# A cross network on one core: six full products ahead of a table-driven run of row products, and output stores cut in four and spaced

## The chip, the cores and the metric

The kernel runs on one core of one Trainium2 chip. A time is device microseconds (us) of one execution. The time before is the median of three runs; beside it stands one execution that was taken with the hardware profiler, and all rows below are from that one.

Engines are named as the profile names them. PE is the matrix engine and PEld its weight loads. DVE is the vector engine, ACT the activation engine, POOL the general one. SP issues the DMA transfers and is in order: a transfer that waits for something holds all transfers behind it.

## The reference, cut to what matters

```python
B, F, D, L = 16384, 26, 16, 6
Din = F * D                      # 416
def reference(x0, ws, bs):       # x0 [16384, 416], ws [6, 416, 416], bs [6, 416], bf16
    x = x0
    for l in range(6):
        proj = jnp.einsum('bd,de->be', x, ws[l]) + bs[l]
        x = x0 * proj + x
    return x
```

Each of six layers is a 416 x 416 product over 16384 rows, a bias, a multiplication by the input and an addition.

## The kernel before, in words

**Tiles.** The 16384 rows are eight groups of 2048; a group is four chunks of 512 rows. Activations lie turned: features on the partitions, batch rows along the free side. 416 features are three tiles of 128 and a rest of 32, the tail. One job is a (group, layer) pair; a job has three output tiles of four chunks, and a tail. One output chunk of 128 x 512 in one PSUM bank sums over 416 features: three times 128 and once 32.

**Two ways to multiply.** A full product (`full`, L694) has 128 feature rows, 128 output features and 512 batch columns. A row product (in `stream`, L1153 and, for the last 32 features, L1157) has 32 feature rows in one of four row quarters of the array, at `tile_position=(r*32, 0)`. Four row products, one in each quarter, run side by side and go to four different banks. A chunk needs 13 of them: three in each quarter, and one more in the quarter that holds the chunk's tail.

**The first part.** Up to the tile `s_lo`, which is tile 1 of job (0, 2), tiles are made with full products and a few short ones (`first_job`, `two_tiles`, `full`, `rows32`).

**The run.** From `s_lo` on everything is one searched order, the string `ORDER`. Each letter says which of the chunks in work (its age) gets its turn in which row quarter; that turn is then all the row products of this chunk in this quarter, three or four. `replay` walks the string in ticks, 20 to a row product (`SLOT`), and gives each row product a place in PE's order and each chunk a bank. It holds model costs: how long a bank is read (`READ`, `NEXT`, `BACK`), and when each of the eight banks is free at the start (`banks`). The last four chunks of the run (`keep`) begin the last job's outputs, which are made in natural layout. `|` in the string is a tail block: the tails of three jobs at once (L741 x36 and L729 x12, two jobs in the last one), there are 15 of them.

**Evictions.** When a chunk is complete, ACT moves it from PSUM to a `tw` buffer with the bias (L595); there are four `tw` buffers of four chunks. For each pair of chunks DVE multiplies by x0 (L607) and adds x (L615). Tails go through ACT (L661) or DVE (L657), and then two short DVE operations (L663, L665). L665 of some jobs adds a copy of the old tail that has been moved by some quarters (`prefill`, `rotate`: two DMA transfers, L487 and L488, put on SP's queue when the tail block one layer earlier has been written out).

**Output and input of groups.** When job (g, 5) is done, `output` turns its tiles back by DMA transposes (L945, L952) into one buffer `ost`, POOL spreads the tail (L980), and `store` (L987) sends the whole group, 1664 KB, to memory in one transfer. The transposed tail of a newly loaded group, `Tb`, lies in the same buffer, so its load (L438) waits for the store. `load_group` is called for groups 5, 6 and 7 from the list `later` at the end of the tail block after which the group's buffers come free; for groups 6 and 7 two thirds of the load (L427, eight transposes) are issued with the output already. After `Tb` come four more transposes (L427), four copies out of `Tb` (L462), and a moved copy of the result (L487, L488).

Of the kernel before, what the change touches and what calls it, by code (L numbers as in the profile page):

```python
# [5 lines left out]
T32 = 32  # L6
# [15 lines left out]
class Program:  # L22
# [192 lines left out]
ORDER = (
    "ABCDMBCTZOELBaAjZSIfFiQPVKHYBCcTVIDSJATKBQLWBQXKNALCZQLWBQCbMRLWBITWBQPCZMLWRALSBQLCRIbCRAPeJYWH"
    "N|AWPJQGDQBDWNITCJnQCZTIWBLQWNALWBQXCNIDWZIDWJYTCRbIWBLQBSbINWHAVCTUBOQLBaTARaDQZOLUSBDUORbICJbA"
    "aVTMGBPYBWPIRaHAORDYKBXQKBTIWBDUOZITCZIOTFADeRYPCNIbWQFPK|ABPWAVKPQBCPQVKDAVePQBKfMRaHJAbSIBKTAZ"
    "SLcNHCBQXBSMLBaAOXZQKHMVSDBQOXBMKXAVKDQVKDBMebUJOHAVObIRCLQBSfJ|EODBTAOZACbVcPKFAeXRYGPBYWPRAKPQ"
    "BiLMRGDNACbNAaXNISHBYCTNYCbVISPFAePBUKDVQaDRIOXFAOXBAObVQGLBcCXNAePZIWTFASPBcKPRUGDNAWDNQXCJAbWR"  # L220
    "APSJYDaRUDSJUfOF|ITCRIODJAbSJATJCQDOBPcWJDIeVbQOFXAVODUKBXQKBTIBaLQCZTAOQZLWFPAWNDUCNTUBOTIBaLQN"
    "WALVCQXBOQLBaTINWDIVODUCNXAOJXAWJDUeYBXOIZHSUBTOIBbCMZDWIZTO|EBPWQBOLAVCPQVKfMFSDARWPANXCUNSDIBS"
    "XYBTKAReLMVSbIBKTAhSLYNHCBQXNCMLWBAaPQVKDQBaPBUKjMZSXEBSPAZKPQVHCBQWDMRKXBIWDVAOXJAWfYJTCQZOLEBW"
    "DcRCTMJWbERKP|ABPWQBKPAVCPQVKDANebUBKXQNaHJASXIBKTAhSLYNHCBQXNCMLWBAaXQNKHAZWTMBKDYRKXNAWDNQXBOQ"
    "BObIRWDQBOTICfZAXaRIPFCYPBaUPCMVaLBIWDVQCPRICfJAebJUSPFAaPQVGL|MBDSNAPKBAObRUGLBAeXNYKHVAWTJAKTY"
    "BLCYRWDRIOXBIWPBUOLRAKbBAWPZQCLRYCbNIWTBISPBYKPRAeDQVPKAJXCURCPQJaDIBafQVGPBMaXRIOH|ABTOAZKPQBKD"
    "BUPaAVKbQdCbMRWLEBWTARKPYBWDNQKDZISXBIOTBAOfRYKDZQLWBQKXARKXMBWLBQCPZAWbJQGDQZWPBIWPQBOLAVCPQVKj"
    "MFSDARWPANXCUNSLEBSDYRCTIBafIVOTE|BPWRALOBcDOZQKXBIDVaITCRIbBSYLBSIXNaALVOQDKBQXKBITBaQLVOADOZXA"
    "WJAXSJYDSJYXOFQDZOAXBOQXBOQLBaITVCQDSZMLWBIXSBQLOBIbCZQLCZITWBQLBaITNWALVCUTBSATNaIDJWYTBSPAdOXY"
    "SF|AODVPAKNYXCBQXaJcHORAPaRIHCBUbCRMLWBIWTBQKPVALWRMGDBQCbRMWLBAWbNAKPZUCXQJaPBIWPBcKPVAWLMRCLBQ"  # L230
    "XCRMLWFAWTBQCPZAaPJAWbJMSDZcPCNXYSF|AOTBPAaBYSPJUGDdQODJMbWBIXOdAXKNQHCBQWDMRCbJAaTVIODJAfaUBXSc"
    "NKHAZSXIBLCVYLSNEXCMBWPIBWLAVCXQBOTAdaPUBOLQVaHJAbCMZSLUBSLARKfARWLMBKDYRCPRIbWBQXJOALBaQVCPISXB"
    "ASPYVKHMBCbNQeDJMSXZIP|FCATBaQPBOIDaVIDSJYDSZMXGJTASBjMCNULCVITBeQLNWADaRXMCJDYSBQPaJAbWRAjSJUPG"
    "dQLOBAPSBYPCVIPSBIDSVYDKRAbeJMXGBXMCVIPSBcLORALiNAXOJQDCNUTBOAXBeQPaBYLOVALWdMTGBYfSVMLG|ABWPAVK"
    "PQBCPVQCPJAebVAWLNQaHBYOXBUOLAVKbMRGDBQWDMRKXAJCbQVOLEBaXABOTYVGLMRWDIBSXIBTKAZSLMBKDQZKXARWDQNX"
    "KBISXNADOBcWbBMSXIZGDRYCTZIWPBIWfNQGLB|AWPRAKPBUCPRUKDJAbeJQPWFICXBUPChMLWFAWTBQKPVAWLNQCLBQCbMR"
    "WDJMWDVISPFAObBUCPVQKfNALWBQWLNACbRMLCYJTWARLW|AJTMWDJUCTVICTJWADVaMTBaNIDKVYTOBAfaNQLVGMTCJMSDA"
    "BXa"
)


def replay(tails, events, needs, keep):

    n = len(tails)
    size = [[3 + (r == tails[c]) if c < n - keep else 2 * (r == tails[c]) for r in range(4)] for c in range(n)]
    free, flight, begun, act = [0] * 4, {}, 0, 156
    banks = [(0, 0), (0, 1), (0, 2), (0, 3), (84, 4), (84, 5), (178, 6), (178, 7)]
    home, read, out, latest, due = {}, {}, [], [[]] * 4, list(events)

    def over(now):  # L260
        nonlocal act
        for end, q, c in sorted((end, q, c) for c, (left, end, q) in flight.items() if not left and end <= now):
            del flight[c]
            if c < n - keep:
                start = max(act, end + READ)
                act, read[c] = start + NEXT, start + BACK
                banks.append((start + BACK, home[c]))
        banks.sort()

    for letter in ORDER:  # L270
        if letter == "|":
            now, m = min(free), due.pop(0)
            parts = [(f - now) // SLOT for f in free]
# [36 lines left out]
        latest[r] = [[start + SLOT * k, r, c, home[c]] for k in range(size[c][r])]  # L310
        out += latest[r]
    over(max(free))
    assert begun == n and not flight and not due
# [4 lines left out]
def bass_standalone__cross_network_dcn__recsys_kernel(
# [25 lines left out]
    n = 0  # L344
# [10 lines left out]
    bias = nc.alloc_sbuf_tensor("bias", [P, 4, L], FP32)  # L355
# [14 lines left out]
    add = pr.add  # L370
# [212 lines left out]
    def evacuate_chunk(g, l, i, j, b, read):  # L583
# [11 lines left out]
        add("act", lambda h: h.activation(  # L595
            tw[r][:, j * CH:(j + 1) * CH], bank(b), ACT_F.Identity, bias=bias[:, i, l:l + 1], scale=1.0),
            reads=[("ps", b), "bias"], writes=[("tw", r, j)])
# [123 lines left out]
    def tails(batch, corners_last=False, banks=None):  # L721
# [220 lines left out]

# [29 lines left out]
    def spread(eng):  # L972
# [6 lines left out]
        else:  # L979
            add(eng, lambda h: h.tensor_copy(dst, sp_), **kw)  # L980

    def store(g, j0, j1):

        rows = out[g * GC + j0 * CH:g * GC + j1 * CH, :]
        o = ost[:, j0 * KK:j1 * KK, :].rearrange("p (j k) f -> p j k f", k=KK)
        pat = "(j p k) f -> p j k f" if g == 0 else "(j k p) f -> p j k f"
        add("sp", lambda h: h.dma_start(rows.rearrange(pat, j=j1 - j0, k=KK), o),  # L987
            reads=[("ost", t, j) for t in range(NT + 1) for j in range(j0, j1)],
            writes=[("out", g, j0)], lane=f"out{j0}", batch=g)
# [119 lines left out]
    def stream(run):  # L1109
# [23 lines left out]
        for _, r, c, b in plan:  # L1133
# [11 lines left out]
                start_job(g, l, ahead=False)  # L1145
            count[c] = count.get(c, 0) + 1
            q, ecols = slice(r * T32, (r + 1) * T32), slice(i * P, (i + 1) * P)
            t = seen[c, r] = seen.get((c, r), -1) + 1
            src, stok = x_src(g, l)
            s3, tok3 = x3_src(g, l)  # L1150
            kw = dict(start=count[c] == 1, stop=count[c] == 4 * NT + 1, tile_position=(r * T32, 0))
            if t < NT:
                add("pe", lambda h, l=l, t=t, j=j, b=b, q=q, ecols=ecols, src=src, kw=kw: h.matmul(  # L1153
                    bank(b), wm[l][q, t, ecols], src(t, j, j + 1)[q, :], **kw),
# [29 lines left out]
    for n, it in enumerate(items[:s_lo]):  # L1184
# [180 lines left out]
```

## Time and profile before

| | us |
|---|---|
| median of 3 runs (lowest, highest) | 464.22 (464.11, 464.41) |
| the profiled execution: device time | 464.1 |
| the profiled execution: span from first to last instruction | 462.3 |
| PE busy | 457.0 |
| DVE busy | 403.5 |
| ACT busy | 381.3 |

The clock granted to PE was 0.999 of full speed on the mean. DVE and ACT work beside PE; what counts is where PE is not fed. Device time and span differ by 1.8 us.

### The profile page before, as it was taken

To read this page: it belongs to the slowest core of one execution; us is meant where nothing else is said; L and a number is where in the kernel's file an instruction comes from. 1 tells how busy PE (TensorE), PEld (TensorE's weight loads), DVE (VectorE), ACT (ScalarE), POOL (GpSimd) and SP (SyncE) were. 2 spreads that over 40 slices of the span, in tenths; PEclk is the share of its full clock that TensorE was granted. 3 is DMA by queue.
4 is the path that set the end of the run, shared out by engine and by line. 5 is a ranking of instruction groups with operands and counts; after the bars stand their busy time and mean duration, and the time that the engine had idled before them with its cause. 6 is when DMAs were issued, how large, how long until landed. Compare 5 with 4: busy or idle time off the path is not lost.

```text
span 462.3 us, 17810 instructions
## 1 busy us (share of the span) xinstructions
PE 457.0 (99%) x7985; PEld 262.8 (57%) x7989; DVE 403.5 (87%) x698; ACT 381.3 (82%) x606; POOL 8.1 (2%) x20
## 2 busy tenths in 40 slices
PE   9999999999999999999999999999999999999996
PEld 5344656565655656555665556566555565555552
DVE  2897898988889998898989989898988988989997
ACT  4676889888988889798888979888888888888786
POOL 2000000000000000000000000000000000000010
PEclk9999999999999999999999999999999999999999
DMA  8977869200001859099447955690000088172799
GB/s 226 187 169 123 172 123 169 48 22 12 16 4 41 137 186 188 15 129 225 87 89 127 208 99 101 110 220 19 24 3 4 24 141 294 50 114 64 209 161 315
DMA packets 136160, 53.79 MB, mean 116 GB/s; under 512 B 113674, under 2 KB 134676, under 8 KB 136084
## 3 DMA queue, kind: packets, MB, share of 16 engines
q1 hardware_dynamic: 135928, 52.54, 54.5%
q8 instruction: 62, 1.02, 0.9%
q14 instruction: 14, 0.11, 0.1%
q10 hardware_dynamic: 156, 0.11, 0.1%
HBM read 5.97 MB, written 13.63 MB: 42 GB/s over the span
## 4 chain that ended last, share of the span: by engine, by line
PE 95%; DVE 2%; DMA 1%; ACT 1%; issue 0%; SPq 0%; DVEq 0%
PE ps L1153 74%; PE ps L741 7%; PE ps L1157 6%; PE ps L694 4%; PE ps L688 1%; PE ps L729 1%; DVE x L1279 1%; DVE x L1273 1%; DMA wm<-in_ws_dram 1%; ACT tw L595 1%; PE ps L715 1%; PE ps L839 0%; DVE tw L607 0%; DVE x L615 0%; SPq L784 0%
## 5 line engine op out<-in xcount | busy, mean ns | idle before, releaser
L1153 PE MATMUL ps<-x,wm 32*128 32x512 bf16 x6288 | 372.3, 374 | 0.0
L595 ACT ACTIVATE tw<-ps,bias 128x512 bf16<-128x512 f32 x524 | 327.3, 688 | 47.6 <-PE ps L1153 38.0
L1153 PEld LDWEIGHTS ps<-x,wm 32*128 32x128 bf16 x6288 | 219.2, 92 | 137.5 <-ACT tw L595 3.9
L607 DVE TENSOR_TENSOR tw<-tw,x 128x1024 bf16<-128x1024 bf16 x262 | 177.0, 689 | 40.6 <-ACT tw L595 39.5
L615 DVE TENSOR_TENSOR x<-tw,x 128x1024 bf16<-128x1024 bf16 x262 | 170.8, 687 | 0.3
L1157 PE MATMUL ps<-x,w 32*128 32x512 bf16 x524 | 159.3, 374 | 0.0
L1157 PEld LDWEIGHTS ps<-x,w 32*128 32x128 bf16 x524 | 44.6, 92 | 6.7
L741 PE MATMUL ps<-x,wm 128*32 128x512 bf16 x564 | 33.6, 380 | 0.0
L661 ACT ACTIVATE ts<-ps,bias 128x512 bf16<-128x512 f32 x32 | 20.4, 686 | 13.6 <-PE ps L729 13.6
L559 ACT ACTIVATE tw<-ps,bias 128x1024 bf16<-128x1024 f32 (+1 forms) x22 | 20.4, 1000 | 8.7 <-PE ps L715 7.1
L741 PEld LDWEIGHTS ps<-x,wm 128*32 128x32 bf16 x564 | 13.5, 96 | 18.0 <-ACT tw L595 3.2
L694 PE MATMUL ps<-x,wm 128*128 128x512 bf16 x88 | 20.5, 379 | 0.4 <-issue 0.3
L665 DVE TENSOR_TENSOR x<-ts,x 128x512 bf16<-128x512 bf16 x47 | 18.3, 418 | 0.3
L568 DVE TENSOR_TENSOR tw<-tw,x 128x1024 bf16<-128x1024 bf16 (+1 forms) x21 | 13.2, 637 | 2.0 <-ACT tw L559 1.8
L694 PEld LDWEIGHTS ps<-x,wm 128*128 128x128 bf16 x92 | 8.4, 98 | 10.8 <-issue 1.7
L657 DVE SCALAR_TENSOR_TENSOR ts<-ps,bias,x 128x512 bf16<-128x512 f32 x15 | 11.2, 746 | 3.3 <-PE ps L729 3.3
L573 DVE TENSOR_TENSOR x<-tw,x 128x1024 bf16<-128x1024 bf16 (+1 forms) x21 | 12.6, 633 | 0.0
L663 DVE TENSOR_TENSOR ts<-ts,x 128x512 bf16<-128x512 bf16 x32 | 12.4, 417 | 0.0
L980 POOL COPY ost<-ot 128x512 bf16<-128x512 bf16 x5 | 3.8, 750 | 363.0 <-DMA ot<-x 363.0
L849 DVE COPY x<-ps 128x512 bf16<-128x512 bf16 x6 | 2.4, 421 | 8.0 <-PE ps L839 8.0
L1218 PE MATMUL ps<-wm,x 128*128 128x416 bf16 x48 | 9.3, 340 | 0.0
L1267 ACT ACTIVATE x<-ps 128x416 bf16<-128x416 f32 x16 | 7.7, 528 | 1.5 <-PE ps L1218 1.5
(53 smaller groups left out, 74.5 us busy)
## 6 DMA issues: line engine op xcount, KB each, us to landing
out_dram<-ost SPq DMA_DIRECT2D x6, 1664.0 KB, 7.7
x<-x SPq DMA_DIRECT2D x24, 96.0 KB, 2.1
x<-in_x_dram SPq DMA_DIRECT2D x8, 208.0 KB, 3.6
x<-in_x_dram SPq DMA_DIRECT2D x4, 416.0 KB, 7.4
wm<-in_ws_dram SPq DMA_DIRECT2D x5, 312.0 KB, 3.6
x<-x SPq DMA_DIRECT2D x22, 64.0 KB, 2.3
out_dram<-x SPq DMA_DIRECT2D x3, 416.0 KB, 2.6
out_dram<-ost SPq DMA_DIRECT2D x2, 416.0 KB, 2.9
```

Source lines behind the costliest of these rows:

```text
L559: add("act", lambda h, a=a, w=w, b0=b0: h.activation(tw[r][:, a * CH:(a + w) * CH], psum[:, b0 * CH:(b0 + w) * CH], ACT_F.Identity, bias=b ...
L568: add("dve", lambda h, a=a, e=e: h.tensor_tensor(tw[r][:, a * CH:e * CH], tw[r][:, a * CH:e * CH], x0s[s0][:, i * GC + a * CH:i * GC + e * ...
L573: add("dve", lambda h, a=a, e=e: h.tensor_tensor(xs[so][:, i * GC + a * CH:i * GC + e * CH], tw[r][:, a * CH:e * CH], src(i, a, e), ALU.ad ...
L595: add("act", lambda h: h.activation(tw[r][:, j * CH:(j + 1) * CH], bank(b), ACT_F.Identity, bias=bias[:, i, l:l + 1], scale=1.0), reads=[( ...
L607: add("dve", lambda h: h.tensor_tensor(tw[r][:, o], tw[r][:, o], x0s[s0][:, c], ALU.mult), reads=[("tw", r, k) for k in both] + [x0_tok(s0 ...
L615: add("dve", lambda h: h.tensor_tensor(paired(xs[so][:, c], "p (k j q) -> p j k q"), paired(tw[r][:, o], "p (j k q) -> p j k q"), paired(s ...
L661: add("act", lambda h: h.activation(ts[r][:, :], bank(b), ACT_F.Identity, bias=bias[:, 3, l:l + 1], scale=1.0), reads=[("ps", b), "bias"], ...
L665: add("dve", lambda h: h.tensor_tensor(x3s[so][:, :], ts[r][:, :], res, ALU.add), reads=[("ts", r)] + rtok, writes=[("x3", so), ("x3", so, ...
L694: add("pe", lambda h, t=t, j=j: h.matmul(bank(banks[j]), wm[l][:, t, ecols], src(t, j, j + 1), start=(first and t == 0), stop=(not first a ...
L741: add("pe", lambda h, t=t, j=j, src=src, l=l, b=b, ro=ro, qo=qo: h.matmul(psum[qo, b * CH:(b + 1) * CH], wm[l][:, t, NT * P:D], src(t, j, ...
L1153: add("pe", lambda h, l=l, t=t, j=j, b=b, q=q, ecols=ecols, src=src, kw=kw: h.matmul(bank(b), wm[l][q, t, ecols], src(t, j, j + 1)[q, :], ...
L1157: add("pe", lambda h, l=l, b=b, q=q, ecols=ecols, s3=s3, kw=kw: h.matmul(bank(b), w3[l][q, ecols], s3[q, :], **kw), reads=tok3 + [("w3", l ...
```

## The change

The run starts with six full products. Of its first tile's four chunks, chunk 0 gets none, chunk 1 one, chunk 2 two and chunk 3 all three of its 128-row products in that form (`AHEAD`). The row products that they replace, four each, are left out of the run: 24 of 6812. The last chunk is left with only its tail.

`ORDER` is another string, searched with other starting values: all banks of the run are taken as free 84 to 120 ticks sooner than before, and ACT 120 ticks sooner.

`store` sends a quarter of a group's rows now. For groups 0 to 4, `output` calls it for the first quarter at once. The other three are put in the list `paced` with a count of ACT evictions each: 22, 26 and 30 evictions after the output (`PACE`, `STEP`). `pace` issues such a quarter when the count has been reached, with a dependence on that eviction. While `paced` holds anything, the calls of `load_group` from `later` are held back; `pace` makes them when the last quarter has been put on the queue. Group 5's store, which is not made in `output`, is one transfer as before.

```diff
 SLOT = 20
+PACE, STEP = 22, 4
 FENCE, PHASE, CHANGE = 22, 52, 9
+AHEAD = (0, 1, 2, 3)
 ORDER = (
-    "ABCDMBCTZOELBaAjZSIfFiQPVKHYBCcTVIDSJATKBQLWBQXKNALCZQLWBQCbMRLWBITWBQPCZMLWRALSBQLCRIbCRAPeJYWH"
+    "ABCDDCBYXCjZQNeDmcIVjGPQlWDINCbUJCXIROEDNeDUJPGABbQVKMHBWATOVAPKVQDBWAXROYLFCQXZOAPBeUPZSH|MBCTM"
...
@@ def replay(tails, events, needs, keep):
-    size = [[3 + (r == tails[c]) if c < n - keep else 2 * (r == tails[c]) for r in range(4)] for c in range(n)]
-    free, flight, begun, act = [0] * 4, {}, 0, 156
-    banks = [(0, 0), (0, 1), (0, 2), (0, 3), (84, 4), (84, 5), (178, 6), (178, 7)]
+    whole = [3 - AHEAD[c] if c < 4 else 3 for c in range(n - keep)]
+    size = [[whole[c] + (r == tails[c]) if c < n - keep else 2 * (r == tails[c]) for r in range(4)] for c in range(n)]
+    free, flight, begun, act = [0] * 4, {}, 0, 36
+    banks = [(0, 0), (0, 1), (0, 2), (0, 3), (0, 4), (0, 5), (58, 6), (58, 7)]
@@ in evacuate_chunk
-        add("act", lambda h: h.activation(
+        pace(add("act", lambda h: h.activation(
             tw[r][:, j * CH:(j + 1) * CH], bank(b), ACT_F.Identity, bias=bias[:, i, l:l + 1], scale=1.0),
-            reads=[("ps", b), "bias"], writes=[("tw", r, j)])
+            reads=[("ps", b), "bias"], writes=[("tw", r, j)]))
@@ in tails
-        while later:
+        while later and not paced:
             load_group(later.pop(0))
@@ in output
             turn(g, 2)
-            store(g, 0, NJ)
+            store(g, 0, 1)
+            paced.extend((evicted[0] + PACE + STEP * (j - 1), g, j) for j in range(1, NJ))
@@
+    paced, evicted = [], [0]
+
+    def pace(op):
+        evicted[0] += 1
+        while paced and evicted[0] >= paced[0][0]:
+            _, g, j = paced.pop(0)
+            store(g, j, j + 1).deps.append(op)
+            while later and not paced:
+                load_group(later.pop(0))
@@ in stream
-            t = seen[c, r] = seen.get((c, r), -1) + 1
+            ahead = AHEAD[c] if c < NJ else 0
+            t = seen[c, r] = seen.get((c, r), ahead - 1) + 1
+            whole = 4 * (NT - ahead) + 1
-            kw = dict(start=count[c] == 1, stop=count[c] == 4 * NT + 1, tile_position=(r * T32, 0))
+            kw = dict(start=count[c] == 1 and not ahead, stop=count[c] == whole, tile_position=(r * T32, 0))
...
-            if count[c] == 4 * NT + 1:
+            if count[c] == whole:
@@ before the call of stream
+    _, (g, l), i = items[s_lo]
+    for t in range(max(AHEAD)):
+        full(g, l, i, ring[:NJ], True, True, chunks=[j for j in range(NJ) if AHEAD[j] > t], ts_=[t])
     bka, left = stream(items[s_lo:])
```

More of the change, by code (lines that the diff above doesn't have):

```diff
@@ L219 @@
[L219 to L238, printed above, removed]
+    "ABCDDCBYXCjZQNeDmcIVjGPQlWDINCbUJCXIROEDNeDUJPGABbQVKMHBWATOVAPKVQDBWAXROYLFCQXZOAPBeUPZSH|MBCTM"
@@ new lines @@
+    "VCPCMZDaUNTeAJTaMVKHQBCXQNCPIZSDBUCXRMaLEBSDQdKbAZWTcJGPAVODNUDOJUTCIRODIBSbUBTKMVGDAZWTBQKDQdCb"
+    "IRWPcFCXQZCPIRWDJQWPEBCTAZSPUJCLAZCXMRaLUBWLAVLSgNXGIRCDUNS|IDJTECRODANCfYVKTMFWDUNCPANaXJQODdAT"
+    "OJUCLURODINCbUBCXQNaLEVCTMBaPUBWLMRCLMhCXMJSDIZSPFACTUBSPIVCLUBCXQNaDIZCXIhTaUNH|ANWTIFCDcCVTMJa"
+    "HAWBXAWRLASdLUOBLcOVDUKNbCVIPSBIDSBYTOVIDKVQDSJMXGBAXSZAPKRUDKNUDWNAXKBQXBOgLRWEPBOUZDICTZUCJTMW"
+    "BLMWREDCRXAeBXYSJPEWRDOQLBCcXZSEN|CDQNWDINDCgRbOUFfSIBbiIRDSIBTKYPVCMLBWIDVSIDRKUDBWQbBObIBWQLZO"
@@ new lines @@
+    "UHRCAXdOQLBKQDRaATJOALCZcDWRIbOFULSBcTNCIDSZIPFCUPBWADZWMTBKYPVCMDVacPRGIbWFA|SPBMCPVAPCVgPCNULa"
+    "BULaBQLWZDQKVbMCVAOTJAaLQBKTBcSLAdTKYVCLMVSDINCXYJSPFAODAZOTBYKDVYSLNAKbBYXKQNDKAhTaUBKTMVGDUNSD"
+    "MJTCIZOTABSPUBOLQVCLMRCDQdWbIFS|PBICTVAPSBcPSZALROUDJOUDKVQDJSAfJCQbVCQLNWALNWcTBKQDRaIPBKUPRCAP"
+    "RAaPBWYLRCYLBSYXJCQLVaMBDaMXhSIPBKUPCVMLBWIDVSAPJCYXJCULZSADReMXJGQDRacPFCXMBWM|RCPISFDQDSJACXdQ"
+    "ObBYOLRAaLRUDKRMXCNIDWJYTOBIPCVAPSJUHCAZDaRMXKFYDCcRXaEJTOAZLOBULCAVPYSBPQCNLQCdLMaBLWZMHSBbMCVM"
@@ new lines @@
+    "|RCPISFDQDCNQaXBQCbRMLWBULhOEDNaQXBKQPCdMLBWIDVSIDRKUDJCQbWBLQOVAfBOULRaEPVCUDROULFCAXRaAPJSUDRK"
+    "UPFCUPBWADZWMTBKYPVCMLBacLROALNaQDJOQDhKQPFCrMBWM|RCPISFDQDSJACXdMSbJUHNCUPBWAPRWAPBOUDNcWLZEODV"
+    "YOTBIOBfUKRDSIPBKAZTKUNHAWBTCYDRWYPJCIXZAWDRMeXYJGPUBWPCMVLBWAPVSDMRKDYBOTYJCLQVaEDVSfMFCUPBWAPV"
+    "SDMRKDYBWTYJOXERCM|RCPISFDADaNQXKFgDSZAbOJUTCJQDSZIPFCUPBWAPVSIDRKUDBOYTJWMDVCMfVKQDSJMDaJATKVAf"
+    "JSUDRKPUFCUPBWMLRCAPBaULNCULZCIXRaMHCNYDWNAPJeQXNCM|CPJUSDJMDCNQaXBMSXdAPKRUHCRMDaNITCBcTNWIDVCM"
@@ new lines @@
+    "TBOYLVSALReAbJOUDVKQPFCYPBWAPVSIDRKUDJCYXJCQDZeQPFWIbNSEDNCDYNSIXFCATBaQPJCcDOdUTFaIPVCIDRaULBSI"
+    "XNCAPRCYPJCULBeUDNeQLZWEPRCMbBOUSLNA|BCTUPBWMDdWIDRKcXZOEDNaUTBKQNDKMfBKATaBQPKZEDVSYPBKUPCVMLBW"
+    "IDVSIDRKUDBWQbBObIBWQLZOALVOAXdKQDJSgDRKUPBKMBbCMRDeMZTGUBTWMJDWIRDKQDBWMfBOUbBWMLZCULZSMDZOAPJW"
+    "QbNCM|CPJUSDJMDWJMCXBMSXdAPKRUHCRMDaNITCBcTNWAPVKQDRKMDBOYTJeMXRCIDVSIPFCUPBWAPVSIDRCYPBOYXJSEDR"
+    "aATZKUBTKUNDWIPBKUDVSAPRKAbBWYLNCYLVOAXJOYHBCUTZeI|NCLUOFDMWDBMCXZMKfRUCLRMWDNAaPJAbKRUODNLUCJDY"
@@ L239 @@
+    "CVMbSBMaDYVKPERCbMRWDINCXYJDWIBXCUNTKAdLQCZLQeNHAaNXCUNL|AWBPUBWPAOZDYOVQCPdaDURObEJCbRWMDNTUOAB"
 )
@@ L986, in store @@
         pat = "(j p k) f -> p j k f" if g == 0 else "(j k p) f -> p j k f"
-        add("sp", lambda h: h.dma_start(rows.rearrange(pat, j=j1 - j0, k=KK), o),
-            reads=[("ost", t, j) for t in range(NT + 1) for j in range(j0, j1)],
-            writes=[("out", g, j0)], lane=f"out{j0}", batch=g)
+        return add("sp", lambda h: h.dma_start(rows.rearrange(pat, j=j1 - j0, k=KK), o),
+                   reads=[("ost", t, j) for t in range(NT + 1) for j in range(j0, j1)],
+                   writes=[("out", g, j0)], lane=f"out{j0}", batch=g)
     def spread_pairs():
```

2 lines of the change are left out of this document (removed).

## The prediction

> **What bounds the kernel now.** I read the page's engine totals and its chain first, then the waits, then the chain in order of time.
>
> ```profile
> PE 457.0 (99%) x7985; PEld 262.8 (57%) x7989; DVE 403.5 (87%) x698; ACT 381.3 (82%) x606; POOL 8.1 (2%) x20
> PE 95%; DVE 2%; DMA 1%; ACT 1%; issue 0%; SPq 0%; DVEq 0%
> ```
>
> PE is busy 457.0 of 462.3 us and is 95% of the chain that ended last. So the time is PE's work, plus what little PE loses. The next rows, from the waits, say what weight loads waited for.
>
> ```profile
> PEld ps L1153 <- ACT tw L595: 3.9, 20, 0.2
> PEld ps L821 <- DMA wm<-in_ws_dram: 0.5, 1, 0.5
> PEld ps L1153 <- DVE ts L657: 0.2, 1, 0.2
> ```
>
> The waits on ACT are 0.2 us each and mostly lie beside running products. No row of the run waits on a DMA: L821 is in the start-up. One wait, on L657, is kept for later.
>
> How well does PE run inside the run? Time from one tail block to the next comes from the chain in order of time, the number of products from windows over the lines of the row products (first L1153, then L1157).
>
> ```profile
> 57.58 2.06 PE ps L741 x36
> 86.72 2.06 PE ps L741 x36
> 106.98 2.06 PE ps L741 x36
> 189.59 2.06 PE ps L741 x36
> 240.30 2.06 PE ps L741 x36
> 267.46 2.06 PE ps L741 x36
> ```
>
> ```profile
> 40.20:57.50 17.30, 17.22 (x288) 10.30 (x288) 1.00 0.62 138
> 59.90:86.64 26.74, 26.72 (x454) 16.35 (x454) 1.00 0.69 127
> 89.00:106.90 17.90, 17.84 (x303) 9.86 (x303) 1.00 0.06 16
> ...
> 40.20:57.50 17.30, 7.13 (x23) 1.85 (x23) 1.00 0.62 138
> 59.90:86.64 26.74, 11.34 (x38) 3.27 (x38) 1.00 0.69 127
> 89.00:106.90 17.90, 7.86 (x25) 2.13 (x25) 1.00 0.06 16
> ```
>
> The three stretches hold 311, 492 and 328 row products. From block to block 492 products and one block take 86.72 - 57.58 = 29.14 us, 328 and one block 20.26 us. The difference, 8.88 us over 164 products, is 54.1 ns for one, so 217 ns for four side by side. This is the full rate of the array, as the full products show below: inside the run there is nearly nothing to win.
>
> ```profile
> 37.53 2.76 PE L694 MATMUL ps<-x,wm 128*128 128x512 bf16 x12
> 40.23 0.83 PE L1153 MATMUL ps<-x,wm 32*128 32x512 bf16 x12
> 57.51 2.12 PE L741 MATMUL ps<-x,wm 128*32 128x512 bf16 x36
> 59.92 0.61 PE L1153 MATMUL ps<-x,wm 32*128 32x512 bf16 x8
> 86.65 2.13 PE L741 MATMUL ps<-x,wm 128*32 128x512 bf16 x36
> ```
>
> These timeline rows give the start of the first stretch: 40.23 to 57.51 is 17.28 us for 311 products, and 311 x 54.1 ns is 16.83: 0.45 us is lost. The second, 59.92 to 86.65, is 26.73 us against 26.62: 0.11 us, which every stretch pays. So the first stretch loses 0.34 us more than another one. That is what a better start can win.
>
> **The change, part by part.**
>
> *Six full products for 24 row products.* From 37.53 to 40.23, 12 full products take 2.70 us, 0.225 each with the seam to what follows; without it they can't be under the 0.217 of four row products by much. Six cost 1.30 to 1.35 us, the 24 that go 24 x 54.1 ns = 1.30 us. Sum: 0, and 0.05 against it at most. The seam from full to row products is there before and after. The Trainium skill has another price: in "TensorE: Matmul & The Clock Gate", Part 3 ("Measured speedup vs the span model"), four row tiles give 3.07 times the speed of one, not four. By that rule 24 row products would cost 1.69 us (an estimate) and the exchange would win 0.39 us; the trace, with 217 ns for four, does not agree, and the measurement decides.
>
> *The start of the run.* The chunks of the first tile become complete one after another instead of together, so banks return earlier and ACT starts sooner; the 0.34 us can go. Lower end 0, upper end 0.34. I take 0.3, near the upper end, since the chunks then alternate in the first stretch as they do in the others.
>
> *The new string elsewhere.* Its number of products and blocks is the same. In the built program the sixth, eighth and ninth tail blocks come after 2559, 3391 and 3859 row products, where before 2519, 3363 and 3819 stood ahead; with the 24 in full form that is 64, 52 and 64 later. At 54.1 ns, less 0.3, these blocks come 3.2, 2.5 and 3.2 us later. Cost by itself: 0, with plus or minus 0.2 from the 0.11 us that stretches pay. The last block comes 44 products later, 2.1 us nearer to the end; its tail is written at 438.55 and the last job's first use of it is L1099.
>
> ```profile
> 438.55 0.75 DVE L665 TENSOR_TENSOR x<-ts,x 128x512 bf16<-128x512 bf16 x2
> 444.97 0.33 PE L1099 MATMUL ps<-w,x 32*128 32x416 bf16 x1
> ```
>
> There are 5.7 us between them, so 3 remain. Cost 0.
>
> *Stores in four.* SP's part of a store is 0.4 us; three more for five groups are 6 us on SP, which waits most of the time. PE waits for no store. The Trainium skill ("DMA: Bandwidth & Descriptors", "Rules for kernel authors") asks for one large transfer where many small ones can be coalesced; here the landing of a store is off PE's path, so that rule costs nothing by itself.
>
> *What waits behind the quarters.* This is the part that can cost. The held-back `load_group` moves from behind a tail block's copies to before them. In the built order of SP, after group 1's output: first quarter, eight L427, three quarters, four transposes into `Tb`, four L427, four copies, two copies of the loaded tail, and only then the moved tail of job (3, 4). Before, that moved tail stood right behind the eight L427. SP before:
>
> ```profile
> 210.00 0.40 SPq L987 DMA_DIRECT2D out_dram<-ost  x1
> 210.44 14.37 SPq L427 DMA_TRANSPOSE x<-in_x_dram  x8
> 224.86 0.59 SPq L487 DMA_DIRECT2D x<-x  x1
> 228.29 5.18 SPq L438 DMA_TRANSPOSE ost<-in_x_dram  x4
> 243.51 0.53 SPq L487 DMA_DIRECT2D x<-x  x1
> ...
> 244.72 0.59 SPq L487 DMA_DIRECT2D x<-x  x1
> ```
>
> The moved tail of (3, 4) is the row at 224.86. Its user is the first L665 behind the eighth tail block; the block is the one at 240.30:
>
> ```profile
> 242.97 0.74 DVE L657 SCALAR_TENSOR_TENSOR ts<-ps,bias,x 128x512 bf16<-128x512 f32 x1
> ...
> 243.96 0.42 DVE L665 TENSOR_TENSOR x<-ts,x 128x512 bf16<-128x512 bf16 x1
> ```
>
> ```profile
> out_dram<-ost SPq DMA_DIRECT2D x6, 1664.0 KB, 7.7
> out_dram<-ost SPq DMA_DIRECT2D x2, 416.0 KB, 2.9
> out_dram<-ost SPq DMA_DIRECT2D x1, 832.0 KB, 4.3
> x<-x SPq DMA_DIRECT2D x24, 32.0 KB, 1.9
> x<-x SPq DMA_DIRECT2D x24, 96.0 KB, 2.1
> ```
>
> Now the sum. The first quarter leaves at 210.0 + 3.2 = 213.2. Issue 0.4. The eight transposes take 14.4 us behind a 1664 KB store; the four of the same size at 228.29 take 5.18, so eight undisturbed 10.4. Behind a quarter I take 11.4 (ends 10.4 and 14.4). The three quarters, 1248 KB, lie between 832 KB (4.3) and 1664 KB (7.7): 6.0 to landing. By the fit that the Trainium skill gives in "DMA: Bandwidth & Descriptors", "Anatomy of one DMA" (2.0 us and 436 GB/s, there for the other kind of issue), it would be an estimated 4.9. From the first `Tb` transpose to the copies of the loaded tail is 243.51 - 228.29 = 15.2; those and the two that now follow are 0.6 each, 1.9 until the last is issued, and 2.1 to its landing: 19.2 in all. 213.2 + 0.4 + 11.4 + 6.0 + 19.2 = 250.2, with ends 247.5 and 254.9. L665 is ready at 243.96 + 2.5 = 246.5. So DVE, which is in order, stands still 3.7 us (1.0 to 8.4) in this one place, where it doesn't before.
>
> What hides it: ACT has four `tw` buffers, 16 evictions of about 0.7 us, so it doesn't feel 4 us. But behind the ninth tail block PE needs the bank that L657 reads, and L657 stands behind DVE's backlog; the wait of 0.2 us on L657, quoted first, says that PE has no time to spare there. The backlog shrinks by DVE's idle time up to then:
>
> ```profile
> 246.30:270.00 23.70, 19.91 (x33) 1.00 1.02 176
> ...
> 269.96 0.75 DVE L657 SCALAR_TENSOR_TENSOR ts<-ps,bias,x 128x512 bf16<-128x512 f32 x1 [0.90 <-PE ps L729]
> ```
>
> 23.7 - 19.9 = 3.8 us. A standstill of 3.7 us is just used up, at a cost of 0; each us beyond 3.8 is a us of PE. At the late end the cost is 8.4 - 3.8 = 4.6 us. Group 2's load does the same to the moved tail of job (5, 2), but the output there leaves some 6 us later in a stretch that has 46 us from store to use instead of 34; I find 2 us to spare, and take 0.
>
> *Sum.* 0 - 0.3 + 0 + 0 + 0 = -0.3 on the profiled execution's own 464.1 us, which is 463.8; I allow 0.1 for the seam and the edge of the string. The median before is 464.22, 0.1 above that execution, so the median after is about 464.0.
>
> **The rivals.**
>
> *Slower: the moved tail of (3, 4) comes too late.* Place and mechanism as above. It decides from a standstill of 3.8 us on. At 5.5 us, the middle of the late half, PE loses 1.7 us: 464.2 - 0.3 + 1.7 = 465.6. For it: the margin is as good as zero in my own sum. Against it: PE can have some tenths to spare in this block, and the transposes may run nearer to 10.4.
>
> *Slower: the new string pays more per stretch.* It hands banks over in other places. If half of the 15 stretches lost as much more as the first one does now (0.34), that is +2.5 us less 0.3: 466.4. Against it: the 54.1 ns held in stretches of 328 and 492 products alike.
>
> *Nothing happens.* The start's loss is only moved into the full products' seam: 464.2.
>
> *Faster than forecast.* The store's burst is gone from the DMA queues. For it: eight transposes at 14.4 instead of 10.4 us. Against it: no PE row in the run waits on a DMA. It would have to free a quarter of the 3.9 us that weight loads wait on ACT as well: -0.3 - 1.0, 462.9.
>
> **How the numbers follow.** About 0.2% of the time, 0.93 us, is what a measurement of this kernel can tell from no change. My forecast and the case that nothing happens both lie within it, together with standstills up to 5 us: 0.68 (0.55 for the forecast, 0.1 for nothing, 0.03 for the full products at the skill's price, 463.6). The late tail is 0.19, the dearer string 0.07: 0.26 slower. The faster case has 0.06. The range starts at 463.6, where all of the start's loss is won and stretches gain 0.2, and goes to 465.6, the middle of the late tail. It leaves out about 0.06 below and 0.14 above. The forecast's own range is 463.6 to 464.6.
>
> **What would show it.** Right: the first stretch of the run takes as little per product as the second; behind the eighth tail block the first or second L665 waits on a DMA x<-x by some 4 us; DVE then runs without idle time up to the ninth block; PE shows no wait there over 0.3 us. Wrong: a PE wait of a us or more on L657 behind the ninth block (about 271 us); stretches with over 55 ns per product; waits of ACT on DVE; or no wait of L665 at all, which would mean that SP got through sooner than I think.

## The result, and the profile after

The kernel after takes 470.43 us (median of 9 runs, 465.74 to 475.66), the one before 464.23 in the same session (464.11 to 464.51). The ratio is 1.0107, with a 95% interval of 1.0085 to 1.0128: 1.07% slower; it leaves out, as a slow state, the two slowest executions of after, 473.03 and 475.66 us, so it is smaller than that of the medians. The profiled execution is the slowest of the nine, 475.66 us with a span of 473.9, so its losses below are larger than those of most. 2.3 us of that span lie ahead of what is changed: the last full products before the run begin at 39.87 instead of 37.53.

Line numbers of after are 2 higher than before's around the evictions (L597, L609, L617, L659, L667), 16 in the run (L1169, L1173), and 14 at the store (L1001).

From the page of after: totals, the chain, and the group of POOL's tail copies (busy and mean ns, then the idle time before it).

```profile
PE 463.2 (98%) x7971; PEld 262.2 (55%) x7971; DVE 402.6 (85%) x698; ACT 380.7 (80%) x606; POOL 25.9 (5%) x20
PE 87%; DMA 4%; DVE 4%; SPq 4%; ACT 0%; issue 0%; DVEq 0%
L983 POOL COPY ost<-ot 128x512 bf16<-128x512 bf16 x5 | 22.1, 4426 | 356.1 <-DMA ot<-x 356.1
```

PE had 95% of the chain before and has 87% now; DMA, DVE and SP's queue took 12%. POOL is busy 25.9 us instead of 8.1, and all of that is in five copies that do what they did before.

The waits of after (total, times, longest):

```profile
DVE x L667 <- DMA x<-x: 14.0, 3, 8.4
DVE x L617 <- DMA ost<-x: 0.9, 1, 0.9
PEld ps L1169 <- DVE ts L659: 4.4, 3, 3.9
PE ps L1169 <- DVE ts L659: 3.4, 1, 3.4
```

The predicted wait of DVE on a moved tail is there, and there is a second, longer one. PE waits on L659 too, but not where the prediction looked for the sign that it is wrong: behind the ninth tail block (272.94) its weight loads wait 0.3 us, and the long wait, in the last two rows, lies behind the eleventh (330.95). The timeline tells the story in order. SP's queue first:

```profile
214.71 0.41 SPq L1001 DMA_DIRECT2D out_dram<-ost  x1
215.16 11.88 SPq L429 DMA_TRANSPOSE x<-in_x_dram  x8
227.09 2.04 SPq L1001 DMA_DIRECT2D out_dram<-ost  x3
234.21 6.10 SPq L440 DMA_TRANSPOSE ost<-in_x_dram  x4
...
251.11 0.59 SPq L489 DMA_DIRECT2D x<-x  x1
...
276.89 0.38 SPq L1001 DMA_DIRECT2D out_dram<-ost  x1
277.33 12.18 SPq L429 DMA_TRANSPOSE x<-in_x_dram  x8
289.55 2.08 SPq L1001 DMA_DIRECT2D out_dram<-ost  x3
...
313.50 0.59 SPq L489 DMA_DIRECT2D x<-x  x1
```

Group 1's store opens it at 214.71. The moved tail of job (3, 4) begins with the row at 251.11; its second transfer, L490, lands at 253.74. Now the timelines of DVE and of POOL in after (in brackets the idle time before a row):

```profile
247.69 0.75 DVE L659 SCALAR_TENSOR_TENSOR ts<-ps,bias,x 128x512 bf16<-128x512 f32 x1
248.36 0.42 DVE L665 TENSOR_TENSOR ts<-ts,x 128x512 bf16<-128x512 bf16 x1
253.83 0.42 DVE L667 TENSOR_TENSOR x<-ts,x 128x512 bf16<-128x512 bf16 x1 [5.06 <-DMA x<-x]
...
275.64 0.70 DVE L609 TENSOR_TENSOR tw<-tw,x 128x1024 bf16<-128x1024 bf16 x1
276.24 0.76 DVE L659 SCALAR_TENSOR_TENSOR ts<-ps,bias,x 128x512 bf16<-128x512 f32 x1
...
316.07 0.42 DVE L667 TENSOR_TENSOR x<-ts,x 128x512 bf16<-128x512 bf16 x1 [8.43 <-DMA x<-x]
...
327.48 1.29 DVE L617 TENSOR_TENSOR x<-tw,x 128x1024 bf16<-128x1024 bf16 x2 [0.94 <-DMA ost<-x]
```

```profile
208.49 0.94 POOL L983 COPY ost<-ot 128x512 bf16<-128x512 bf16 x1 [50.62 <-DMA ot<-x]
261.62 15.19 POOL L983 COPY ost<-ot 128x512 bf16<-128x512 bf16 x1 [52.18 <-DMA ot<-x]
322.69 4.33 POOL L983 COPY ost<-ot 128x512 bf16<-128x512 bf16 x1 [45.88 <-DMA ot<-x]
```

DVE stands still 5.06 us, until 253.83. From there to 276.24 it has no gap: it works off its backlog, multiplications and additions of two SBUF tiles one behind the other. POOL's copy of group 2's tails begins at 261.62, in the middle of that, and ends at 276.81: 15.19 us for what takes 0.94 one group earlier. It ends 0.57 us after L659 began, which reads PSUM. The store of group 2 waits for this copy and leaves at 276.89. SP is in order, so what stands behind it, the load of group 7 and then the moved tail of job (5, 2) at 313.50, is late too: DVE stands still 8.43 us, and the next copy on POOL (322.69, 4.33 us) falls into the next backlog.

The windows of the stretches (PE, PEld, DVE, ACT and POOL busy, then granted clock, DMA share and GB/s), after first, then before:

```profile
261.00:277.00 16.00, 16.00 (x301) 8.99 (x293) 16.00 (x27) 13.54 (x23) 15.19 (x1) 1.00 0.46 66
330.00:340.00 10.00, 6.56 (x111) 2.82 (x107) 9.97 (x18) 4.81 (x9) 0.00 (x0) 0.89 0.50 158
340.00:350.00 10.00, 10.00 (x148) 5.10 (x143) 7.57 (x14) 6.22 (x10) 0.00 (x0) 0.77 0.11 28
```

```profile
250.00:266.00 16.00, 16.00 (x302) 9.22 (x298) 14.71 (x24) 14.20 (x23) 0.62 (x1) 1.00 1.08 193
```

DVE was busy 14.71 of 16 us before, and POOL's copy took 0.62 there; it is busy 16.00 of 16 while the copy takes 15.19. Behind the second standstill PE is busy 6.56 of 10 us, and in the 10 us after that its granted clock is 0.77: 148 matrix instructions, where the row of before has 302 in 16 us, or 189 in 10. The Trainium skill ("TensorE: Matmul & The Clock Gate", Part 1) says that PE's clock drops to half after an idle window of about 3.4 us and comes back after as long a busy one. The trace agrees that it fell and came back, but not to the us: PE stood 3.44 us, up to 338.52, and its clock was at half from 337.7 to 344.6, which makes the means of 0.89 and 0.77; so it came back only 6.0 us after PE had gone on. And a wait of this length did not always bring the clock down: in experiment 7 PE stood 3.48 us and the clock stayed at 1.00.

To price places, I took from each trace the time from one tail block to the next, less 54.0 ns for each row product between them and 2.41 us for the block. This "excess" is what a stretch loses. The rest of the table is the excess of the run's first stretch, the time from the last block to the end of PE, less its products, and the time from PE's end to the end of the span.

```
                     first    sum of 14   of that in the stretches     behind the   PE's end to
                     stretch  later ones  to the blocks 10, 11, 12     last block   span's end
before               0.49     2.0         0.13  0.17   0.13            14.11        3.85
after                0.16     11.1        0.32  2.33   6.75            14.17        4.27
```

In after the loss begins in the stretch that ends with the tenth block and is 9.1 us in all.

### The profile page after: what moved, and what is told of

Read it like the earlier page. It is cut to its first block, busy times and chain, and to the rows that moved or that the text cites. A ratio compares the mean times of both kernels' runs of the same rounds, so it can differ in the third digit from the quotient of the medians.

```text
span 473.9 us, 17799 instructions
## 1 busy us (share of the span) xinstructions
PE 463.2 (98%) x7971; PEld 262.2 (55%) x7971; DVE 402.6 (85%) x698; ACT 380.7 (80%) x606; POOL 25.9 (5%) x20
## 4 chain that ended last, share of the span: by engine, by line
PE 87%; DMA 4%; DVE 4%; SPq 4%; ACT 0%; issue 0%; DVEq 0%
PE ps L1169 65%; PE ps L743 6%; PE ps L1173 6%; PE ps L696 5%; DVE x L617 2%; DVE tw L609 2%; PE ps L1237 2%; DMA out_dram<-ost 1%; PE ps L690 1%; SPq L429 1%; SPq L440 1%; PE ps L731 1%; DMA wm<-in_ws_dram 1%; DMA ost<-x 1%; PE ps L841 1%; PE ps L717 1%
## 5 line engine op out<-in xcount | busy, mean ns | idle before, releaser
L1169 PE MATMUL ps<-x,wm 32*128 32x512 bf16 x6264 | 374.6, 377 | 5.3 <-DVE ts L659 3.4
L597 ACT ACTIVATE tw<-ps,bias 128x512 bf16<-128x512 f32 x524 | 327.0, 688 | 55.6 <-PE ps L1169 43.8
L1169 PEld LDWEIGHTS ps<-x,wm 32*128 32x128 bf16 x6264 | 217.7, 92 | 147.0 <-ACT tw L597 7.5
L609 DVE TENSOR_TENSOR tw<-tw,x 128x1024 bf16<-128x1024 bf16 x262 | 176.2, 691 | 36.7 <-ACT tw L597 35.2
L617 DVE TENSOR_TENSOR x<-tw,x 128x1024 bf16<-128x1024 bf16 x262 | 171.3, 689 | 1.4 <-DMA ost<-x 0.9
L1173 PE MATMUL ps<-x,w 32*128 32x512 bf16 x524 | 155.4, 377 | 0.0
L1173 PEld LDWEIGHTS ps<-x,w 32*128 32x128 bf16 x524 | 43.5, 93 | 6.2 <-issue 0.2
L983 POOL COPY ost<-ot 128x512 bf16<-128x512 bf16 x5 | 22.1, 4426 | 356.1 <-DMA ot<-x 356.1
L667 DVE TENSOR_TENSOR x<-ts,x 128x512 bf16<-128x512 bf16 x47 | 18.6, 421 | 14.4 <-DMA x<-x 14.0
L696 PE MATMUL ps<-x,wm 128*128 128x512 bf16 x98 | 23.9, 395 | 0.0
L659 DVE SCALAR_TENSOR_TENSOR ts<-ps,bias,x 128x512 bf16<-128x512 f32 x15 | 11.2, 749 | 1.9 <-PE ps L731 1.9
L851 DVE COPY x<-ps 128x512 bf16<-128x512 bf16 x6 | 2.4, 422 | 10.4 <-PE ps L841 10.4
L853 ACT ACTIVATE x<-ps 128x512 bf16<-128x512 bf16 x6 | 3.3, 595 | 7.3 <-PE ps L841 7.3
```

Of the source, the lines that this page charges most:

```text
L597: pace(add("act", lambda h: h.activation(tw[r][:, j * CH:(j + 1) * CH], bank(b), ACT_F.Identity, bias=bias[:, i, l:l + 1], scale=1.0), rea ...
L609: add("dve", lambda h: h.tensor_tensor(tw[r][:, o], tw[r][:, o], x0s[s0][:, c], ALU.mult), reads=[("tw", r, k) for k in both] + [x0_tok(s0 ...
L617: add("dve", lambda h: h.tensor_tensor(paired(xs[so][:, c], "p (k j q) -> p j k q"), paired(tw[r][:, o], "p (j k q) -> p j k q"), paired(s ...
L667: add("dve", lambda h: h.tensor_tensor(x3s[so][:, :], ts[r][:, :], res, ALU.add), reads=[("ts", r)] + rtok, writes=[("x3", so), ("x3", so, ...
L696: add("pe", lambda h, t=t, j=j: h.matmul(bank(banks[j]), wm[l][:, t, ecols], src(t, j, j + 1), start=(first and t == 0), stop=(not first a ...
```

## The experiments

All ratios are to the kernel before on the same chip, whose median there was 464.7 us in three sessions.

**1. The lead and the string, with whole stores.**

```diff
-            store(g, 0, 1)
-            paced.extend((evicted[0] + PACE + STEP * (j - 1), g, j) for j in range(1, NJ))
+            store(g, 0, NJ)
```

> The change without its stores: six full products and the new string, each group's store in one transfer as before. Theory (moved tails come late because the quarters hold back the load, which then stands ahead of them on SP): no late moved tail, no DVE standstill, the start's 0.3 us is won: 463.9 us, 463.6 to 464.3. Rival A (the new string itself loses time between tail blocks): 466 to 470. Rival B (three more transfers per group disturb the DMA queues): 463.9 as well.

Measured: 465.25 us, 1.0012 (1.0003 to 1.0021). Of the 1.07% only a ninth is left, so the quarters make nearly all of the loss. But I had expected a gain: lead and string alone cost about 0.55 us. In the account above: first stretch 0.155 (0.33 won), later stretches 2.49 (0.48 lost, 0.32 of it in the stretch to block 11), behind the last block 14.23 (0.12 lost), end of span 4.14 (0.29 lost). Together +0.56.

**2. The quarters alone, with the string of before.**

```diff
 ORDER = (
-    "ABCDDCBYXCjZQNeDmcIVjGPQlWDINCbUJCXIROEDNeDUJPGABbQVKMHBWATOVAPKVQDBWAXROYLFCQXZOAPBeUPZSH|MBCTM"
...
+    "ABCDMBCTZOELBaAjZSIfFiQPVKHYBCcTVIDSJATKBQLWBQXKNALCZQLWBQCbMRLWBITWBQPCZMLWRALSBQLCRIbCRAPeJYWH"
...
-AHEAD = (0, 1, 2, 3)
```

> The change's stores alone, with the old string and no full products ahead. In this build the last quarter of group 1 falls behind the tail block, so that the moved tail of job (3, 4) stands ahead of the held-back load again; the one of job (5, 2) stands behind it, with some 2 to 4 us to spare. Theory: 464.2 us, 464.0 to 464.6. Rival A (the string): 464.2. Rival B (quarters disturb by themselves): 466 or more.

Measured: 464.87 us, 0.9998 (0.9989 to 1.0007). Four stores for one cost nothing. In this string the last quarter comes after the tail block, so the moved tail of (3, 4) is still ahead of the load, and DVE doesn't wait on it. The moved tail of (5, 2) stands behind its load, and there L666 waits 0.15 us (304.57). The loss needs both parts: the quarters that hold the load back, and the string that lets the load go before the moves.

**3. Quarters and new string, the load behind the moves.** `pace` issues a held-back load only for group 5; those of groups 6 and 7 wait for the next tail block's end.

```diff
-            while later and not paced:
+            while later and not paced and later[0] == 5:
                 load_group(later.pop(0))
```

> The change whole, but pace releases only group 5's load; the loads of groups 6 and 7 come at the end of the tail block as before, behind the moved tails. One condition is added. Theory: no standstill of DVE on a moved tail, POOL's copies under 1.1 us each, 463.9 us (463.6 to 464.3), which would be a version faster than before by 0.3. Rival A: 466 or more. Rival B: 466 or more.

Measured: 465.38 us, 1.0013 (1.0003 to 1.0022). The standstills are gone, and so are the long copies on POOL: the view of its line has shortest, median and longest in ns. Group 2's store leaves at 262.10, by SP's timeline:

```profile
L983 POOL COPY ost<-ot x5: 613/715/1031, 155.0 to 377.1; 128x512 bf16<-128x512 bf16 x5
```

```profile
262.10 0.39 SPq L1001 DMA_DIRECT2D out_dram<-ost  x1
```

What is left is as much as with whole stores, so within the intervals the place of the load is the whole of the quarters' cost. The gain that I expected here is not there, as in experiment 1.

**4. Without POOL's copy for groups 2 to 4.**

```diff
-            spread("pool")
+            if g < 2:
+                spread("pool")
```

> The change, but POOL's spread of the tail into the store buffer is left out for groups 2 to 4 (their last 32 output columns are then those of group 1). It tells whether POOL's long copy is the link between the first and the second standstill. Theory: DVE still stands some 5 us on the moved tail of job (3, 4) near 249 us, but group 2's store leaves near 264 instead of 277 us, the moved tail of job (5, 2) is in time within 1 us, and the time is 463.9 to 465.5. If the long copy is only an effect of something else that delays the store: 468 to 471, as with the change whole.

Measured: 465.92 us, 1.0037 (1.0016 to 1.0057). The wait of DVE, and SP's timeline at the store of group 2:

```profile
DVE x L667 <- DMA x<-x: 5.5, 1, 5.5
```

```profile
266.54 0.39 SPq L1002 DMA_DIRECT2D out_dram<-ost  x1
```

The first standstill is about as long as in after, 5.5 us instead of 5.06, but the store leaves 10.4 us sooner, and there is no second standstill. The first standstill by itself costs 0.64 us (the stretch to block 10 has an excess of 0.77 instead of 0.13). So in these profiles it is the copy that turns 0.6 us into nine; by the medians it is 1.2 us over before without the copies and 6.2 with them. The time is 0.4 us above my range. Four of the ten executions took 466.83 to 469.67 us; what these lost was not profiled.

**5. Whole stores, but the loads ahead of the moves.** As in experiment 1, with the loads of groups 6 and 7 put in front of `prefill` in `tails`.

```diff
+        while later and later[0] != 5:
+            load_group(later.pop(0))
...
-        while later and not paced:
+        while later and later[0] == 5:
             load_group(later.pop(0))
```

> As e1_one_store (new string, one transfer per group), but the loads of groups 6 and 7 are put ahead of the tail block's moved tails on SP, as the change has them. Only the three later quarters and the wait for their landing are missing against the change. Theory (the order alone costs little; the quarters' landing, about 7 us between the eight transposes and Tb, makes the moved tail late): DVE stands 0 to 2 us on the moved tail of (3, 4), the copy on POOL stays near 1 us, the time is that of e1, 465.2 (464.8 to 465.8). If the order alone is enough: a standstill of 4 us or more, and 466 to 471.

Measured: 465.41 us, 1.0019 (1.0007 to 1.0030); the standstill is 0.6 us. With one store the load of `Tb` follows the eight transposes at once (226.62), while in after it waits 7.1 us for the quarters to land. Order alone is not enough for the loss: the load must also be late, as it is behind the last quarter.

**6 and 7. Which of the two loads?** Only group 6's goes behind the moves, or only group 7's.

```diff
-            while later and not paced:
+            while later and not paced and later[0] != 6:
```

> The change, with only group 6's load put behind the moved tails; group 7's load stays ahead of the moved tail of (5, 2). Theory (the second standstill is a consequence of the first, through POOL's long copy and the late store): with the first gone, no second one over 1 us, and 465.4 as e3. If the second standstill stands by itself: DVE waits some 8 us near 305 us and the time is 467 to 471.

Measured: 465.15 us, 1.0012 (1.0003 to 1.0021), no standstill in the whole kernel. With no first standstill, group 7's load, which stays ahead of its moves, does no harm.

```diff
-            while later and not paced:
+            while later and not paced and later[0] != 7:
```

> The change, with only group 7's load put behind the moved tails; group 6's stays ahead of the moved tail of (3, 4). Theory: the first standstill of 5 us stays, POOL's copy for group 2 is long in the runs where DVE works off its backlog without a gap, and the store leaves up to 14 us late; but the moved tail of (5, 2) does not wait for it, so there is no second standstill. 465.4 + 0.6 = 466.0 (465.3 to 467.0). If the first standstill alone makes the loss: 468 to 471.

Measured: 472.29 us (4 runs), 1.0164 (1.0146 to 1.0182), much more than my 465.3 to 467.0. Its waits, and the timelines of POOL, DVE and SP where group 2's output is made:

```profile
DVE x L667 <- DMA x<-x: 6.9, 1, 6.9
DVE x L617 <- DMA ost<-x: 6.0, 2, 4.0
```

```profile
262.11 15.19 POOL L983 COPY ost<-ot 128x512 bf16<-128x512 bf16 x1 [54.04 <-DMA ot<-x]
276.72 0.76 DVE L659 SCALAR_TENSOR_TENSOR ts<-ps,bias,x 128x512 bf16<-128x512 f32 x1
277.38 0.39 SPq L1001 DMA_DIRECT2D out_dram<-ost  x1
```

Again 15.19 us, and again the copy ends 0.58 us after L659 began. Here the moved tails of the next block are in time, but DVE then waits for tile buffers: the output transposes that must read them (`ost<-x`) are late, since SP is 15 us late. The stretches to the blocks 10 and 12 lose 2.0 and 3.7 us. So the second standstill is no cause of its own; once SP is this late, whatever it brings next is waited for.

**8. The last tail block earlier.** Experiment 1 and experiments 3 and 6 have no standstill but end later: 4.14, 4.86 and 4.83 us from PE's end to the span's end instead of 3.85. In the new string the last tail block is 44 products later. Here, on top of experiment 3, its mark is put 24 letters sooner.

```diff
-    "CVMbSBMaDYVKPERCbMRWDINCXYJDWIBXCUNTKAdLQCZLQeNHAaNXCUNL|AWBPUBWPAOZDYOVQCPdaDURObEJCbRWMDNTUOAB"
+    "CVMbSBMaDYVKPERCbMRWDINCXYJDWIBX|CUNTKAdLQCZLQeNHAaNXCUNLAWBPUBWPAOZDYOVQCPdaDURObEJCbRWMDNTUOAB"
```

> e3 with the last tail block moved 24 letters earlier in the string, some 4 us earlier on PE; all products stay. Theory for the 0.6 us by which e3 and e1 are slower than before though their start is 0.33 us shorter: the last block comes 2.1 us nearer to the end, so the tail's transpose for group 6 falls between the last output transposes on SP, which are back to back there, the last stores leave later, and the time from PE's last product to the end grows from 3.85 us to 4.1 to 4.9 us. Then the end is back at 3.8 to 4.0 us and the time is 464.6 (464.2 to 465.0) beside a kernel before of 464.75. If the place of the block has nothing to do with it: 465.2 to 465.6 and an end of over 4.1 us.

Measured: 465.39 us, 1.0015 (1.0006 to 1.0024), end 4.58. The end is 0.3 us shorter than in experiment 3, but not 3.8 to 4.0, and the time is the same: the block's place is not the cause.

**9 and 10. The last store of group 6 left out**, from experiment 3's kernel and from the kernel before. It has 832 KB, not the 416 that the expectations say.

```diff
     nat_store(0, 0, NJ)
-    store_pairs(1, 0, KK)
     for kk in range(1, KK):
```

> The kernel with the new string, quarters and the load behind the moves, less the last 416 KB store of group 6, so these rows of the output are not written. Theory, the last stores of the kernel stand behind that store in the DMA queues: from the end of PE to the end of the span 3.8 us instead of 4.86, and 464.3 us. Rival, the backlog comes from the turns of group 6, which are late with this string whatever is stored: 4.6 us or more, and 465.2.

> The kernel before, less the same store; the same rows are not written. If that store isn't in the way of the last ones before, as their landing of 1.67 us says, the end stays at 3.8 us and the time at its own, ratio 0.9995 to 1.000. If it is in the way there too, the end falls by as much as it does with the new string.

Measured: 464.51 us, 1.0001 (0.9991 to 1.0010), and 464.68 us, 0.9993 (0.9984 to 1.0002). The last DMA of the kernel, 104 KB, with its time to landing, in experiment 3, then without that store, then in before without it:

```profile
out_dram<-x SPq DMA_DIRECT2D x1, 104.0 KB, 2.7
```

```profile
out_dram<-x SPq DMA_DIRECT2D x1, 104.0 KB, 1.7
```

```profile
out_dram<-x SPq DMA_DIRECT2D x1, 104.0 KB, 1.7
```

From PE's end to the span's end it is 4.86, 3.86 and 3.85 us; with the store, before had 3.85 as well. SP's rows of the last two stores, in before and in experiment 3:

```profile
453.83 0.37 SPq L1003 DMA_DIRECT2D out_dram<-ost  x1
455.45 4.67 SPq L1286 DMA_DIRECT2D out_dram<-x  x4
```

```profile
455.53 0.37 SPq L1017 DMA_DIRECT2D out_dram<-ost  x1
455.94 4.60 SPq L1305 DMA_DIRECT2D out_dram<-x  x4
```

PE ends at 458.42 and 458.74. Before, the store in question (`store_pairs(1, 0, KK)`, L1003 and L1017) leaves 4.6 us ahead of that, and 1.6 us ahead of the next store. In experiment 3 it leaves 3.2 us ahead, and the next store 0.4 us behind it. So with the new string the queues still work on it when the last outputs come, which takes 1.0 us; before, they are done with it in time, and leaving it out wins nothing that can be told from zero. Other profiles agree: with the store 4.6 us ahead of PE's end in experiment 2 the end is 3.86, with 3.9 us in experiments 1 and 11 it is 4.14, with 3.5 us in experiment 8 4.58, and with 3.05 us in experiment 5 4.95. Experiment 11 has the string of before, so the lead alone also moves this store; why was not pursued.

**11. The lead with the string of before.** Same turns in the same order, less the three that have no products left; whole stores. If it had kept the start's gain, it would have beaten both kernels.

```diff
 ORDER = (
-    "ABCDDCBYXCjZQNeDmcIVjGPQlWDINCbUJCXIROEDNeDUJPGABbQVKMHBWATOVAPKVQDBWAXROYLFCQXZOAPBeUPZSH|MBCTM"
...
+    "ABCDMBCTZELBaAjZSIfFiQPKHYBCTVIDSJATKBQLWBQXKNALCZQLWBQCbMRLWBITWBQPCZMLWRALSBQLCRIbCRAPeJYWHN|AW"
...
```

> The six full products are put ahead of the string of before: same turns in the same order, less the three turns of chunk 3 that have no products left (its last turn, the tail, is put where its first stood). Stores are whole. Theory, the start wins 0.33 us and it is the new string that gives back more: the first stretch as cheap per product as the others, the later stretches and the end as before (2.0 us and 3.9 us), ratio 0.9993, 464.4 us beside a kernel before at 464.7. Rival, the lead shifts everything behind it and that by itself costs: ratio 1.0010, 465.2.

Measured: 466.04 us, 1.0033 (1.0021 to 1.0044). Its start, from PE's timeline, then the windows over the two lines of the row products; and the same of after:

```profile
37.82 4.06 PE L696 MATMUL ps<-x,wm 128*128 128x512 bf16 x18
41.81 0.39 PE L1168 MATMUL ps<-x,wm 32*128 32x512 bf16 x3
58.64 2.13 PE L743 MATMUL ps<-x,wm 128*32 128x512 bf16 x36
```

```profile
41.75:58.55 16.80, 16.74 (x264) 9.04 (x264) 1.00 0.60 130
...
41.75:58.55 16.80, 6.53 (x23) 1.99 (x23) 1.00 0.60 130
```

```profile
39.87 4.06 PE L696 MATMUL ps<-x,wm 128*128 128x512 bf16 x18
43.86 0.39 PE L1169 MATMUL ps<-x,wm 32*128 32x512 bf16 x3
58.92 0.40 PE L743 MATMUL ps<-x,wm 128*32 128x512 bf16 x4
```

```profile
43.80:58.85 15.05, 14.99 (x253) 8.24 (x253) 1.00 0.76 155
...
43.80:58.85 15.05, 6.79 (x23) 1.88 (x23) 1.00 0.76 155
```

Here 287 products take 16.83 us, 1.30 more than 287 x 54.1 ns. In after 276 take 15.06, 0.13 more. Before lost 0.45. So neither of my two theories was right: the later stretches of this kernel lose 2.0 us, as before, but the start loses 0.85 us more instead of 0.33 less, and the end is 4.14 us instead of 3.85. The lead pays only with a string that was made for it. No kernel of this study beats the one before.

## Why the prediction was wrong

464.0 us was forecast, 470.43 measured, outside the range of 463.6 to 465.6.

**Six full products: right.** 18 full products take 41.81 - 37.82 = 3.99 us, 0.222 each; the six cost 1.33 us, the 24 row products 1.30.

**The start of the run: right.** The first stretch loses 0.13 us instead of 0.45, a gain of 0.32 (0.3 forecast). Experiment 11 adds that the gain belongs to the lead and the string together, while I had put it down to the lead. (Of the string's starting values only those of four banks are sooner than before, by 84 and 120 ticks, and ACT's; the other four banks start at zero in both.)

**The new string elsewhere: wrong, by 0.9 us.** "Cost by itself: 0, with plus or minus 0.2." With whole stores the stretches lost 0.48, the part behind the last block 0.12, and the end of the span 0.29 (1.0 in experiment 3's profile). The step priced the stretches and the last block's tail, and left out the end: what lead and string do to the stores that stand ahead of the last outputs. Experiments 9 and 10 show that part: without one store the ratio falls from 1.0013 to 1.0001 with the new string, and from 1 to 0.9993, which can't be told from 1, with the old. The rival of the dearer string had the sign, but neither the place nor the 2.5 us.

**Stores in four: right as it stands.** 0.9998 in experiment 2.

**What waits behind the quarters: right in place, mis-sized, and then not followed to the end.** The step's chain held: eight transposes 11.88 us (11.4 taken), the wait on the first L667 behind the eighth block, DVE without a gap to the ninth, and no wait of PE over 0.3 us there. The standstill was 3.7 by the sum and measured 5.06 in after. One term behind the eight transposes was short: from the issue of the three quarters to the load of `Tb` it took 234.21 - 227.09 = 7.1 us, not 6.0. The cover of 3.8 us was too small. Standstills of 5.06, 5.52 and 6.91 us (after, experiments 4 and 7) cost 0.19, 0.64 and 2.04 us in the stretch to block 10, each 4.9 us less: each us beyond the cover is a us of PE, as the step says, but the cover is 4.9 us. Had this been all, the time would have been experiment 4's 465.92. That this is close to the late-tail rival's 465.6 is luck: that rival has 1.7 us from the standstill and a gain of 0.3 from the start, where the runs show 0.6 us from the standstill and 0.55 lost by lead and string.

The sentence that failed is the next one: "Group 2's load does the same to the moved tail of job (5, 2) ... I find 2 us to spare, and take 0." It treated the first standstill as over when DVE had worked it off. But group 2's output is made just while DVE works it off, and needs a copy on POOL. The copy took 15.19 us instead of 0.7 and made SP's whole queue late by as much. That cost 2.2 and 6.6 us in the stretches to the blocks 11 and 12; of the 6.6, 3.4 are PE's wait and 3.0 are the 6.0 us that it then ran at half speed. POOL, 2% busy, was in no term of the sum.

Shown by runs: without the first standstill the copies take 0.6 to 1.1 us (experiments 3 and 6); with the standstill but without the copy the loss is 0.6 us (4); with both the stretches to the blocks 10 to 12 lose 9.0 us in after and 5.7 in experiment 7, whichever load comes next, where they lose under 0.05 without either. Not shown is why the copy did not get in at once; the last section says how often it did.

## What to carry to other kernels

A moved transfer is to be followed past the first wait that it causes: ask what starts while the late engine catches up, and which queue stands behind that. An engine that is busy 2% can carry the critical path if an in-order queue waits for it. And a searched order fits the start that it was searched for: the same lead won 0.3 us at the start with one order and lost 0.85 with another.

## What the runs showed of the hardware

A copy from SBUF to SBUF on POOL of 128 x 512 bf16 and DVE's operations with two SBUF inputs hold each other up. The profiles of all 13 kernels have 62 such copies, and 50 of them began while DVE ran one operation right behind the other. Of these, 44 took under 1.2 us, and in 42 of them it was DVE that waited: its next multiplication or addition took 1.1 us instead of 0.68. Group 1's copy in after, at 208.49, is one of them; two additions otherwise take 1.29 us together:

```profile
208.28 1.70 DVE L617 TENSOR_TENSOR x<-tw,x 128x1024 bf16<-128x1024 bf16 x2
```

No multiplication or addition of this size took over 0.85 us in any profile except beside a copy on POOL.

The other six copies did not get in: 15.19 us twice, and 3.80 to 4.33 us four times (one in after, one in experiment 10, two in experiment 11). They ended when DVE next let go. Both copies of 15.19 us ended within 0.6 us of the start of DVE's next operation on PSUM; the 4.33 us copy at 322.69 ended at 327.02, in the 0.94 us gap that DVE had before 327.48; the other three ended in DVE's next gap or within 0.4 us of it. So how long DVE goes on without a gap says how long a copy can take that does not get in, and a standstill makes such a stretch long. Whether it gets in is another matter, and what decides that is not shown. It may be why executions of after lie between 465.74 and 475.66 us, but only one of them was profiled.

The Trainium skill ("SBUF — State Buffer", "SBUF: two separate sides") has the mechanism: DVE and GpSimd share a pair of ports as an exclusive lock, which a DVE operation with two SBUF inputs holds for its whole length. The traces agree that POOL, which that page calls GpSimd, and DVE exclude each other. What that section does not lead one to expect is that the lock did not come free for POOL between some 25 DVE operations. That it is this lock, and not something else that DVE's operations do, is argued from the starts and ends of copies and operations.
